# Moving ten of sixteen K transposes from TensorE to the DMA crossbar, and halving the chunk extremes in fp16

## The chip, the cores and the metric

The kernel runs on one core of one Trainium2 chip. Times are device microseconds (us) of one execution. The profile is taken on one of those executions; its span (first to last instruction) is some 2 us shorter than the device time. TensorE, VectorE, ScalarE, GpSimd and SyncE are the engines; in profile lines they are PE (PEld is its weight loads), DVE, ACT, POOL and SP. A letter q after an engine's name is its queue issuing something. "L170" is a source line. The changed kernel's line numbers are those of the kernel before plus 7, past the change.

## The reference, cut to what matters

```
q, k, v: (4, 8, 768, 64) float32     # batch, heads, rows, head size
k_min, k_max = min and max of k over chunks of 32 rows        # 24 chunks
ub  = sum_d max(q*k_min, q*k_max)        # bound per query row and chunk, causal chunks only
sel = the 6 chunks of largest bound
attn = softmax(q k^T / 8, masked to sel and to the causal triangle) ;  x = attn v
x -> (4, 768, 512)                       # heads side by side
h = relu(x @ w_in);  u, v = halves of h;  v_n = layer norm of v
out = (u * (w_spatial @ v_n + b_spatial)) @ w_out
```

## The kernel before

Sixteen pairs of heads pass through the attention part, and the second part ("MLP" below, one round per batch entry of four pairs) is woven between them. Each pair's K (768 rows x two heads of 64) lies in SBUF with rows on partitions and must be transposed: the chunk extremes are reductions along rows, and the scores need it as an operand.

```python
ps_ml = ctx.enter_context(tc.psum_pool(name="ps_ml", bufs=3))   # shared with the MLP

def k_transpose(self):
    if self.i < 16:                                   # all pairs
        self.kT = kT = ps_ml.tile([P, S], F16, tag="mlp", name="kTp")
        for t in range(NQT):                          # 6 blocks of 128 x 128
            nc.tensor.transpose(kT[:, t * P:(t + 1) * P], self.k[:, t], identity)
    else:
        self.kT = sb.tile([P, S], F16, tag="kT", name="kT", bufs=3)
        nc.sync.dma_start_transpose(out=..., in_=...)  # K rows x (6 blocks) -> kT

def k_max(self):                                      # k_min likewise, negated
    nc.vector.tensor_reduce(self.kmm[:, 0, :], self.kT.rearrange("d (c ch) -> d c ch", ch=CHUNK),
                            axis=AX.X, op=Alu.max)

def k_operand(self, hi):                              # two copies per pair: the scores' operand
    ...
    copy(self.kh[hi][d0:d1], self.kT[d0:d1])

# [...] already on the DMA crossbar, in SyncE's queue: a (selection and queries, pairs >= 8),
#       xT (attention result, pairs 4 to 14), gT (gated MLP values). The out stores stand there too.

def triangle(self, hi):                               # pairs >= 4: causal triangle on GpSimd
    if self.b == 0: return
    ...
    nc.gpsimd.affine_select(out=blk, in_=blk, compare_op=Alu.is_ge, fill=0.0, ...)

# [...] all loads are issued by GpSimd too: they cast float32 to fp16
tiles["k", g] = sb.tile([P, 2, NQT, 2, D], F16, tag="k", name="k", bufs=3)
nc.gpsimd.dma_start(out=t[...], in_=source(k, b, h, 2))               # pieces of 64 fp16 = 128 bytes
nc.gpsimd.dma_start(out=ws_raw[:, j], in_=moe_w_spatial[j*P:(j+1)*P]) # pieces of 768 fp16 = 1536 bytes
nc.gpsimd.dma_start(out=w_out_sb[:, j], in_=moe_w_out[j*P:(j+1)*P])   # pieces of 1024 bytes
```

In the traces below each engine's instructions run in the order of the program. And the profile counts all the transfers on the same 16 DMA engines of the core.

The softmax here doesn't subtract the row's maximum and nothing guards it: scores larger than these inputs give would overflow.

## Time and profile before

| | before |
|---|---|
| device time, median of 3 | 208.53 us (208.47 to 208.60) |
| profiled span, granted clock | 206.9 us, 1.0 in every slice of the page |

The page's first part gives busy time, share of the span and instructions of each engine.

```profile
PE 187.8 (91%) x1922; PEld 115.1 (56%) x1922; DVE 154.5 (75%) x454; ACT 158.1 (76%) x326; POOL 80.5 (39%) x100
```

The table by stretches gives for each stretch its length, the busy time of each engine with its instruction count, the granted TensorE clock, the time of the DMA packets as a share of 16 engines (over 1 where packets overlap), and last the GB/s that DMA moved.

```profile
core 0: us, PE busy (x) PEld busy (x) DVE busy (x) ACT busy (x) POOL busy (x), PEclk, DMA share, GB/s
57.00:77.00 20.00, 19.39 (x248) 13.47 (x247) 18.72 (x66) 17.68 (x38) 11.39 (x13) 1.00 1.84 134
77.00:97.00 20.00, 20.00 (x221) 12.39 (x220) 18.62 (x54) 15.52 (x33) 8.72 (x10) 1.00 1.84 135
97.00:122.00 25.00, 25.00 (x252) 14.89 (x251) 21.70 (x65) 23.44 (x53) 5.37 (x6) 1.00 1.40 176
122.00:152.00 30.00, 30.00 (x309) 17.82 (x308) 24.09 (x75) 23.82 (x51) 5.18 (x6) 1.00 0.64 122
```

From 77 us TensorE (first number after the length) is busy 75 of 75 us: here only less TensorE work would help. The same view for the time of the loads:

```profile
38.00:50.00 12.00, 10.72 (x171) 8.13 (x168) 10.99 (x39) 11.47 (x24) 9.15 (x12) 1.00 1.77 170
50.00:62.00 12.00, 11.06 (x145) 7.57 (x144) 10.60 (x33) 11.28 (x25) 11.28 (x14) 1.00 2.10 170
62.00:78.00 16.00, 15.45 (x191) 10.56 (x188) 15.02 (x52) 13.73 (x30) 7.39 (x8) 1.00 1.74 127
```

TensorE is not full from 38 to 50 us.

The groups by shape (busy us, mean ns of one, then idle time before and what ended it) show what the change touches: the transposes of K, the maximum, and the copies.

```profile
L170 PE MATMUL kTp<-identity,k 128*128 128x128 f16 x96 | 8.8, 230 | 5.9 <-DMA k<-in_k_dram 5.7
L178 DVE TENSOR_REDUCE kmm<-kTp 128x24 f16<-128x768 f16 x16 | 15.2, 948 | 3.7 <-PE kTp L170 2.7 <-ACT e L271 0.7
L194 DVE COPY kh<-kTp 64x768 f16<-64x768 f16 x30 | 16.5, 549 | 0.5
```

In the page's list of DMA issues the fourteen large K loads have a median of 8.1 us from issue to landing.

### The profile page before, as it was taken

How to read it: one execution, taken by the hardware profiler on the slowest of the kernel's cores; microseconds unless marked ns; L12 is line 12 of the kernel's file. 1: busy time of each engine (PE TensorE's matmuls, PEld its weight loads, DVE VectorE, ACT ScalarE, POOL GpSimd, SP SyncE). 2: the span in 40 equal slices, each digit the busy share in tenths (PEclk: the TensorE clock that was granted, in tenths of full speed). 3: DMA queues.
4: the chain of work that ended last, by engine and by line, in shares of the span. 5: the costliest groups of instructions: out<-in, count | busy, mean ns of one | idle time of the engine just before them, and what ended most of it. 6: DMA issues, size and time to landing. Idle time of an engine off the chain costs nothing.

```text
span 206.9 us, 5068 instructions
## 1 busy us (share of the span) xinstructions
PE 187.8 (91%) x1922; PEld 115.1 (56%) x1922; DVE 154.5 (75%) x454; ACT 158.1 (76%) x326; POOL 80.5 (39%) x100
## 2 busy tenths in 40 slices
PE   0368999898899999999999999999999999999992
PEld 0266776775666665656655656565555454444440
DVE  6467979989799989899797999887647456365520
ACT  4797989899998889785989996669999830666042
POOL 7997659596992463236114111111111110000000
PEclk9999999999999999999999999999999999999999
DMA  5999999999999999979998926648782124540356
GB/s 38 92 118 154 140 178 158 173 177 167 177 162 162 97 119 128 135 130 147 149 278 153 180 62 57 127 88 158 181 166 65 38 29 92 187 152 3 72 128 256
DMA packets 114424, 27.27 MB, mean 132 GB/s; under 512 B 109536, under 2 KB 110816, under 8 KB 114400
## 3 DMA queue, kind: packets, MB, share of 16 engines
q0 software_dynamic: 76544, 12.20, 89.8%
q1 hardware_dynamic: 37856, 14.75, 36.4%
q8 instruction: 15, 0.25, 0.5%
q14 instruction: 9, 0.07, 0.1%
HBM read 24.38 MB, written 6.29 MB: 148 GB/s over the span
## 4 chain that ended last, share of the span: by engine, by line
PE 69%; ACT 17%; DVE 8%; issue 2%; DMA 2%; POOL 0%; DVEq 0%; ACTq 0%; POOLq 0%
PE mlp L388 40%; PE sc L266 12%; ACT e L271 10%; PE acc L289 7%; PE kTp L170 2%; ACT a L257 2%; DVE kmm L178 2%; PE ub L222 2%; DMA k<-in_k_dram 2%; PE trm L251 2%; ACT vraw L398 1%; PE tr L205 1%; DVE vn L412 1%; DVE kmm L182 1%; ACT u L420 1%
## 5 line engine op out<-in xcount | busy, mean ns | idle before, releaser
L271 ACT ACTIVATE e<-sc 128x512 f16<-128x512 f32 x192 | 96.9, 553 | 14.8 <-PE sc L266 13.4
L266 PE MATMUL sc<-a,kh 128*128 128x512 f16 (+3 forms) x256 | 65.5, 308 | 2.1 <-ACT e L271 1.5
L388 PE MATMUL mlp<-w_in_sb,xT 128*128 128x512 f16 x192 | 53.0, 379 | 0.1
L278 POOL TENSOR_SCALAR_AFFINE_SELECT e<-e 128x768 f16<-128x768 f16 x24 | 20.9, 869 | 66.3 <-ACT e L271 66.3
L289 PEld LDWEIGHTS <-e 128*128 128x128 f16 x672 | 31.4, 97 | 17.0 <-DVE x L297 3.8
L388 PE MATMUL mlp<-vn,wsT 128*128 128x512 f16 x144 | 37.3, 379 | 0.0
L289 PE MATMUL acc<-vt,e 128*128 128x65 f16 x672 | 35.3, 193 | 0.7 <-DVE x L297 0.4
L266 PEld LDWEIGHTS <-kh 128*128 128x128 f16 x256 | 22.7, 98 | 13.3 <-issue 0.8
L437 ACT COPY o<-mlp 128x512 f32<-128x512 f32 x24 | 14.1, 586 | 19.5 <-PE mlp L388 19.1
L400 DVE BATCH_NORM_STATS2 stats<-vraw 128x6 f32<-128x512 f32 x24 | 16.6, 693 | 12.9 <-ACT vraw L398 12.5
L388 PE MATMUL mlp<-w_out_sb,gT 128*128 128x512 f16 x96 | 25.1, 379 | 0.0
L388 PEld LDWEIGHTS <-xT 128*128 128x128 f16 x192 | 17.2, 97 | 12.6 <-issue 0.4
L427 DVE SCALAR_TENSOR_TENSOR g<-mlp,b_col,u 128x512 f16<-128x512 f32 x24 | 17.9, 748 | 7.3 <-PE mlp L388 6.2
L232 DVE MAX8 max<-ub 128x8 f32<-128x8 f32 (+4 forms) x160 | 15.6, 165 | 5.1 <-PE ub L222 4.9
L388 PEld LDWEIGHTS <-wsT 128*128 128x128 f16 x144 | 12.9, 98 | 10.4
L178 DVE TENSOR_REDUCE kmm<-kTp 128x24 f16<-128x768 f16 x16 | 15.2, 948 | 3.7 <-PE kTp L170 2.7
L297 DVE TENSOR_TENSOR x<-acc,rec 128x384 f16<-128x384 f32 x32 | 17.6, 551 | 0.4
L336 POOL DMA_DIRECT2D qs<-in_q_dram x14 | 14.6, 1049 | 5.9 <-PE sc L266 5.9
L194 DVE COPY kh<-kTp 64x768 f16<-64x768 f16 x30 | 16.5, 549 | 0.5
L398 ACT ACTIVATE vraw<-mlp 128x512 f32<-128x512 f32 x24 | 14.4, 601 | 3.0 <-PE mlp L388 3.0
L420 ACT ACTIVATE u<-mlp 128x512 f16<-128x512 f32 x24 | 14.3, 598 | 1.7 <-PE mlp L388 1.5
L327 POOL DMA_DIRECT2D k<-in_k_dram x14 | 14.4, 1045 | 2.5 <-PE kTp L170 1.8
(67 smaller groups left out, 230.2 us busy)
## 6 DMA issues: line engine op xcount, KB each, us to landing
out_dram<-o SPq DMA_DIRECT2D x24, 256.0 KB, 2.3
vt<-in_v_dram POOLq DMA_DIRECT2D x8, 384.0 KB, 8.8
k<-in_k_dram POOLq DMA_DIRECT2D x14, 192.0 KB, 8.1
qs<-in_q_dram POOLq DMA_DIRECT2D x14, 192.0 KB, 7.5
ws_raw<-in_moe_w_spatial_dram POOLq DMA_DIRECT2D x6, 192.0 KB, 6.9
w_in_sb<-in_moe_w_in_dram POOLq DMA_DIRECT2D x8, 128.0 KB, 6.9
w_out_sb<-in_moe_w_out_dram POOLq DMA_DIRECT2D x4, 128.0 KB, 7.9
k<-in_k_dram POOLq DMA_DIRECT2D x4, 96.0 KB, 3.4
```

The costliest lines, as they stand in the source:

```text
L178: nc.vector.tensor_reduce(self.kmm[:, 0, :], self.kT.rearrange("d (c ch) -> d c ch", ch=CHUNK), axis=AX.X, op=Alu.max)
L194: copy(self.kh[hi][d0:d1], self.kT[d0:d1])
L266: mm(sc[:, col:col + n], lhsT=self.kh[hi][:, t * P:(t + 1) * P], rhs=self.a[:, q0 // P:(q0 + n) // P, hi, :], start=True, stop=not diag)
L271: nc.scalar.activation(out=self.e[hi][:, g * 512:g * 512 + width], in_=sc[:, 0:width], func=Act.Exp, scale=scale)
L278: nc.gpsimd.affine_select(out=blk, in_=blk, compare_op=Alu.is_ge, fill=0.0, base=0, channel_multiplier=-1, pattern=[[0, NQT], [1, P]])
L289: mm(self.av[:, qi, :], lhsT=self.e[hi][:, c:c + P], rhs=self.v[hi][:, t, 0:D + 1], start=first and n == 0, stop=last and n == len(blocks) ...
L297: nc.vector.tensor_tensor(self.x16[:, :, hi, :], in0=self.av[:, :, 0:D], in1=rec.to_broadcast([P, NQT, D]), op=Alu.mult)
L388: mm(st[group][:, 0:cols], lhsT=lhsT, rhs=rhs, start=(j == 0), stop=(j == n - 1))
L398: nc.scalar.activation(st["vraw"][:, ti, :], h, func=Act.Relu)
L400: nc.vector.bn_stats(stats, st["vraw"][:, ti, :])
L420: nc.scalar.activation(st["u"][:, ti, :], h, func=Act.Relu)
L427: nc.vector.scalar_tensor_tensor(g, in0=vs, scalar=b_col[:, ti:ti + 1], in1=st["u"][:, ti, :], op0=Alu.add, op1=Alu.mult)
```

## The change

The intent: K of pairs 6 to 15 is transposed by the DMA crossbar into SBUF, which frees TensorE of 60 transposes and a PSUM buffer of that use. From SBUF in fp16, the extremes of a chunk of 32 are taken by two elementwise halvings, 32 to 16 to 8, before a reduction over 8.

```diff
         def k_transpose(self):
-            if self.i < 16:
+            if self.i < 6:
                 self.kT = kT = ps_ml.tile([P, S], F16, tag="mlp", name="kTp")
 ...
         def k_max(self):
             self.kmm = sb.tile([P, 2, NCH], F16, tag="kmm", name="kmm")
-            nc.vector.tensor_reduce(self.kmm[:, 0, :], self.kT.rearrange("d (c ch) -> d c ch", ch=CHUNK),
-                                    axis=AX.X, op=Alu.max)
+            self.k_bound(0, Alu.max)
+
+        def k_bound(self, m, op):
+            src = self.kT.rearrange("d (c ch) -> d c ch", ch=CHUNK)
+            if self.i >= 6:
+                for n in (16, 8):
+                    half = sb.tile([P, NCH, n], F16, tag=f"half{n}", name=f"half{n}")
+                    nc.vector.tensor_tensor(half, in0=src[:, :, 0:n], in1=src[:, :, n:2 * n], op=op)
+                    src = half
+            nc.vector.tensor_reduce(self.kmm[:, m, :], src, axis=AX.X, op=op, negate=(m == 1))
 
         def k_min(self):
-            nc.vector.tensor_reduce(self.kmm[:, 1, :], ...same view..., op=Alu.min, negate=True)
+            self.k_bound(1, Alu.min)
```

## The prediction

> **What bounds the kernel now.** The time is 208.53 us, the profiled span 206.9 us, the granted clock 1.0 throughout. The table by stretches shows two regimes. Until about 55 us TensorE is not full (18.6 of 20 us busy from 20 to 40, 14.9 of 17 from 40 to 57), while VectorE (18.4 and 14.9) and ScalarE (17.9 and 16.2) are; the chain of waits alternates there between exponentials, reductions and transposes. From 57 us on TensorE is busy 19.4 of 20 us, then 20 of 20 in each stretch to 152, and the chain of waits is nearly all the MLP's and the scores' matmuls. Those run at pipeline pace: two 128x512 matmuls take 0.43 us in the chain. The matmuls of the stretch 77 to 152, added up at such paces (0.055 us for a transpose, 0.033 for a value matmul), give about 75 us of 75: TensorE throughput is the limit. The end (172 to 203 us) is MLP alone.
>
> **What the change does.**
> - It removes 60 of the 96 K transposes from TensorE. A record shows 219 ns, but six in a row take 0.33 us in the timeline, so 10 pairs x 0.33 = 3.3 us of TensorE time. Pairs 6 and 7 transposed at 45.8 and 53.7 us, in the regime where TensorE is not full; pairs 8 to 15 lie in the full one: 8 x 0.33 = 2.6 us, at par.
> - It frees a PSUM buffer that the MLP shares with the K transposes; TensorE shows no waits for these, so little.
> - VectorE: each 768-wide reduction from PSUM is 0.95 us, two per pair. They become 384- and 192-wide fp16 halvings and a 192-wide reduction. The Trainium skill (VectorE: DVE Perf Modes, "The perf-mode tier table") gives reduce 1x and a 16-bit SBUF tensor_tensor 2x. The trace's 948 ns fits 768 elements at 0.96 GHz (800) plus 148. My estimate on that base is 0.35 + 0.25 + 0.35 = 0.95 us per extreme at worst, 0.7 with a smaller SBUF overhead: a small gain. The two K copies (0.55 us from PSUM) should become about 0.35 us from SBUF. Together 0.4 to 0.9 us less VectorE per pair of about 3.0.
> - It adds ten 196 KB crossbar transposes to the SP queue. Those of x of the same size land in 4.2 us median, up to 8.8 beside the loads. The built order puts five ahead of the first x transpose; with three destination buffers they wait for the K copies three pairs earlier, which the order puts early enough. Slack is some 20 us against under 9: no stall. DMA load rises by about 2 MB of 27 in the crowded first 100 us; K loads arrive well ahead.
>
> **On the critical path.** Of 3.3 us removed, 2.6 lie in the full regime; the built order moves about 1 us of other TensorE work behind the first MLP matmul, but VectorE relief from 45 to 77 us may return it. Expected gain 2 to 3.5 us.
>
> **Prediction.** 205.7 us, 204.0 to 207.8 (8 in 10); faster by over 2%: 0.15, within 2%: 0.82, slower by over 2%: 0.03.
>
> **What would show it.** Right: TensorE still 20 of 20 from 77 us, its busy transposes of K gone, the MLP tail of about 31 us unchanged but starting 2 to 3 us earlier; K extremes' VectorE time equal or slightly less; K copies near 0.35 us; no matmul waiting on kT, a or xT. Wrong: a stall of ScalarE or TensorE on the a transposes (SP head-of-line), halvings slower than 0.35 us, new TensorE gaps from 57 to 100 us because loads or transposes land late, or a gain over 4 us from the freed PSUM buffer.

## The result, and the profile after

| | before, same chip | after |
|---|---|---|
| device time, median | 208.56 us (208.47 to 209.13, 4 runs) | 224.45 us (222.68 to 226.71, 4 runs) |
| profiled span, granted clock | 206.9 us, 1.0 | 222.4 us, 0.974 |

The ratio is 1.073, with a 95% interval of 1.069 to 1.077. Ratios here are the mean time of one kernel's fast runs over that of the other's of the same rounds, so not quite the ratio of the quoted medians. One run of the changed kernel, 226.71 us, counts as slow and is not in the ratio.

The page's first part, after:

```profile
PE 189.4 (85%) x1862; PEld 113.1 (51%) x1862; DVE 151.9 (68%) x494; ACT 158.4 (71%) x326; POOL 80.8 (36%) x100
```

There are 60 matmuls fewer, as intended, but PE busy has not fallen: part of the work ran at half clock (see below). The stretches, in the same columns as before:

```profile
57.00:77.00 20.00, 15.99 (x184) 10.71 (x185) 14.84 (x59) 13.88 (x28) 15.20 (x17) 0.91 2.02 167
77.00:97.00 20.00, 17.69 (x196) 10.70 (x195) 19.18 (x65) 15.46 (x38) 6.39 (x7) 1.00 1.90 147
97.00:122.00 25.00, 19.25 (x188) 10.75 (x186) 19.03 (x74) 17.25 (x39) 6.92 (x7) 1.00 1.39 161
```

TensorE, which should have stayed full, is idle for 4.0 us of 57 to 77, 2.3 of 77 to 97 and 5.75 of 97 to 122. The stretches of the loads:

```profile
38.00:50.00 12.00, 9.37 (x145) 6.72 (x142) 8.78 (x33) 10.21 (x21) 7.21 (x9) 1.00 1.46 128
50.00:62.00 12.00, 6.77 (x76) 4.62 (x73) 5.45 (x23) 5.64 (x13) 6.63 (x8) 0.80 2.42 158
62.00:78.00 16.00, 15.82 (x190) 10.61 (x189) 15.17 (x59) 14.65 (x30) 11.13 (x13) 0.94 2.04 162
```

DMA moves 128 GB/s from 38 to 50 us where the kernel before moved 170, although there is more to move. TensorE works 6.77 us of the next 12, and at a granted clock of 0.80.

VectorE's groups of the change, by shape:

```profile
L185 DVE TENSOR_TENSOR half<-kT 128x384 f16<-128x384 f16 x20 | 7.2, 367 | 6.6 <-DMA kT<-k 6.6
L185 DVE TENSOR_TENSOR half<-half 128x192 f16<-128x192 f16 x20 | 6.3, 324 | 0.0
L187 DVE TENSOR_REDUCE kmm<-half 128x24 f16<-128x192 f16 x20 | 6.7, 341 | 0.1
L201 DVE COPY kh<-kT 64x768 f16<-64x768 f16 x20 | 9.4, 471 | 0.3
```

The median landing time of the K loads has gone from 8.1 to 10.3 us, that of the w_spatial loads from 6.9 to 11.7.

Where does the time go? A good ruler is the start of each triangle selection in GpSimd's timeline, because the 24 of them come in the same order in both kernels.

| triangle selection | before | after | delay |
|---|---|---|---|
| first | 52.9 | 59.9 | 7.0 |
| fourth | 66.1 | 74.0 | 8.0 |
| eighth | 87.3 | 96.1 | 8.8 |
| twelfth | 107.3 | 117.9 | 10.7 |
| thirteenth | 112.2 | 128.6 | 16.5 |
| twenty-fourth | 167.5 | 183.1 | 15.6 |

The delay comes in two jumps, at the first selection and between the twelfth and thirteenth, with a little growth between. After the second jump it no longer grows. The MLP alone at the end lasts 31.53 us in the chain of waits of both kernels.

**First jump.** The chain of waits (start, length, what) runs through a K load and GpSimd's queue to the triangle selection, and only then to TensorE's value matmuls:

```profile
42.76 14.18 DMA k<-in_k_dram
...
57.23 0.37 POOL k L334
...
58.44 1.42 POOL vt L350
...
59.92 0.87 POOL e L285
...
60.83 0.51 PE acc L296 x6
```

The load of k issued at 42.8 us took 14.18 us. The kernel before issued the same load at the same time, and it landed after 7.5 us. The view of waits from 40 to 66 us says who waited (in total, times, longest):

```profile
PEld L296 <- POOL e L285: 5.6, 1, 5.6
PE acc L296 <- POOL e L285: 5.1, 1, 5.1
```

What was new in the machine then: the K transposes of pairs 6 and 7, issued at 38.0 and 39.4 us, which landed only at 48.8 and 52.3 us. The DMA packet records from 38 to 50 us show whom they met: a 1536-byte packet of a w_spatial load took 262 ns on average, against 142 ns before. The typical packet was no slower (median 134 ns, 135 before); 73 of the 362 took over 300 ns, up to 2.1 us, where the kernel before had 4 of 496. So a few packets were held for long. The 128-byte packets of the other loads took 34 and 32 ns on average.

**Second jump.** The chain of waits, later:

```profile
100.00 7.52 DMA gT<-g
...
115.02 0.23 SPq L445
...
115.35 2.86 DMA kT<-k
118.23 0.76 DVE half L185
...
122.13 0.47 DVE x L304
...
122.65 0.66 PE acc L296 x9
```

A gT transpose takes 7.52 us to land. Then pair 15's K transpose starts at 115.35, after an out store (SPq L445); VectorE waits for it; TensorE gets x at 122.6. SyncE's timeline (start, length, what) shows the queue, in which three gT transposes stood from 104.96 on:

```profile
110.23 4.38 SPq L253 DMA_TRANSPOSE a<-qs  x1
114.71 0.54 SPq L445 DMA_DIRECT2D out_dram<-o  x1
115.35 1.26 SPq L173 DMA_TRANSPOSE kT<-k  x1
```

Pair 15's K transpose was behind a selection transpose whose issue held the queue for 4.38 us, and behind the store.

**Half clock.** The records of the granted clock show three windows of 3.4 us at 0.5 in the changed kernel, from 50.3, 60.5 and 121.9 us, each after a gap in TensorE's work. The Trainium skill ("TensorE: Matmul & The Clock Gate", Part 1, the HAM clock gate) tells of windows of 3.4 us and a half clock after an idle one. This trace agrees for the second and third, before which TensorE did nothing for 3.4 us. Before the first it was busy for 1.5 of the 3.4 us, so here the clock fell without an idle window. TensorE was busy for 3.3, 3.1 and 2.7 us of the three, so half speed cost it at most about 9.0 x 0.5 = 4.5 us, by my estimate. So these gaps cost more than their own length.

### The profile page after: what moved, and what is told of

Its sections match the earlier page's. It is cut to its first block, busy times and chain, and to the rows that moved or that the text cites. A ratio compares the mean times of both kernels' runs of the same rounds, so it can differ in the third digit from the quotient of the medians.

```text
span 222.4 us, 5015 instructions
## 1 busy us (share of the span) xinstructions
PE 189.4 (85%) x1862; PEld 113.1 (51%) x1862; DVE 151.9 (68%) x494; ACT 158.4 (71%) x326; POOL 80.8 (36%) x100
## 4 chain that ended last, share of the span: by engine, by line
PE 50%; DVE 21%; DMA 12%; ACT 9%; issue 3%; POOL 2%; SPq 0%; DVEq 0%; POOLq 0%; ACTq 0%
PE mlp L395 31%; DMA k<-in_k_dram 8%; PE sc L273 7%; PE acc L296 6%; ACT e L278 5%; DVE kmm L187 5%; DMA gT<-g 3%; DVE vn L419 3%; DVE half L185 2%; DVE kh L201 2%; DVE x L304 2%; DVE max L239 2%; DMA kT<-k 1%; POOL vt L350 1%; PE ub L229 1%
## 5 line engine op out<-in xcount | busy, mean ns | idle before, releaser
L273 PE MATMUL sc<-a,kh 128*128 128x512 f16 (+3 forms) x256 | 68.0, 316 | 1.0 <-ACT e L278 0.6
L395 PE MATMUL mlp<-w_in_sb,xT 128*128 128x512 f16 x192 | 53.8, 380 | 0.0
L296 PE MATMUL acc<-vt,e 128*128 128x65 f16 x672 | 36.1, 196 | 15.2 <-DVE x L304 9.7
L273 PEld LDWEIGHTS <-kh 128*128 128x128 f16 x256 | 23.2, 100 | 13.2 <-issue 1.2
L395 PE MATMUL mlp<-w_out_sb,gT 128*128 128x512 f16 x96 | 25.9, 388 | 0.0
L239 DVE MAX8 max<-ub 128x8 f32<-128x8 f32 (+4 forms) x160 | 15.9, 162 | 5.7 <-PE ub L229 5.4
L395 PEld LDWEIGHTS <-wsT 128*128 128x128 f16 x144 | 12.9, 97 | 10.7
L350 POOL DMA_DIRECT2D vt<-in_v_dram x8 | 11.5, 1437 | 14.5 <-PE sc L273 12.8
L405 ACT ACTIVATE vraw<-mlp 128x512 f32<-128x512 f32 x24 | 14.3, 595 | 2.8 <-PE mlp L395 2.5
L427 ACT ACTIVATE u<-mlp 128x512 f16<-128x512 f32 x24 | 14.3, 598 | 1.4 <-PE mlp L395 1.3
L419 DVE TENSOR_SCALAR vn<-vraw,mv,rstd 128x512 f16<-128x512 f32 x24 | 12.4, 566 | 2.2 <-ACT rstd L417 2.2
## 6 DMA issues: line engine op xcount, KB each, us to landing
k<-in_k_dram POOLq DMA_DIRECT2D x14, 192.0 KB, 10.3
qs<-in_q_dram POOLq DMA_DIRECT2D x14, 192.0 KB, 10.3
ws_raw<-in_moe_w_spatial_dram POOLq DMA_DIRECT2D x6, 192.0 KB, 11.7
```

Of the source, the lines that this page charges most:

```text
L239: nc.vector.max(self.max8[:, qi - 1, hi, :], ub[:, c0:c0 + CPT * (qi + 1)])
L273: mm(sc[:, col:col + n], lhsT=self.kh[hi][:, t * P:(t + 1) * P], rhs=self.a[:, q0 // P:(q0 + n) // P, hi, :], start=True, stop=not diag)
L296: mm(self.av[:, qi, :], lhsT=self.e[hi][:, c:c + P], rhs=self.v[hi][:, t, 0:D + 1], start=first and n == 0, stop=last and n == len(blocks) ...
L395: mm(st[group][:, 0:cols], lhsT=lhsT, rhs=rhs, start=(j == 0), stop=(j == n - 1))
L419: nc.vector.tensor_scalar(st["vn"][:, ti, :], in0=st["vraw"][:, ti, :], scalar1=st["mv"][:, ti, 0:1], scalar2=st["rstd"][:, ti, :], op0=Al ...
```

## The experiments

Theory A says that the transposes do harm on the DMA side: by being in flight, they delay the loads. Rival B says that the consumers do it: they wait for kT, or the halvings are slow. A was later split: A1 is transposing beside wide load pieces, A2 the extra bytes and their place in the queues, A3 transposing beside loads of any width. D is the rival that transposes anywhere in the program cost time. Eighteen runs were made. All results were correct unless said otherwise. The kernel before, run beside them, took 208.62 to 209.03 us.

### The transposes without a reader, and the halvings alone

e1: the kernel before, plus the ten DMA transposes into tiles that nobody reads.

```diff
-            if self.i < 16:
+            if True:                      # TensorE path for all pairs
+            if self.i >= 6:
+                unread = sb.tile([P, S], F16, tag="kT", name="kT", bufs=3)
+                nc.sync.dma_start_transpose(out=unread..., in_=self.k...)
```

> The kernel before, with the ten DMA transposes of K added into a tile that nobody reads; TensorE still transposes all sixteen pairs, VectorE still reduces from PSUM. Theory A (the DMA side: transposes issued from 38 us on share the 16 DMA engines with the loads, loads land in 14 instead of 8 us, the GpSimd queue stands behind them and the triangle selection of pair 4 comes 7 us late): at least +5 us, 213 to 222, the first triangle selection at 58 to 60 us instead of 52.9. Theory B (the consumer side: VectorE's new order and the halvings cost the time): no change, 208 to 210.

Measured: 223.67 us (223.22 to 224.82), ratio 1.072 [1.069, 1.075]. The first triangle is at 59.5 us (+6.6). The whole loss of the change is there with nobody reading a transpose, so B falls as the main cause. The second half of it is spent differently: with no reader there is no step between the twelfth and thirteenth selections (+15.1 at both). The step is earlier instead, at the ninth (+14.3), where the selection transpose of pair 9 stood in SyncE's queue behind later K transposes and was issued at 100.5 us instead of 86.9.

e3: the changed kernel with the plain 768-wide reductions.

```diff
-            if self.i >= 6:
+            if False:                     # no halvings
```

> The changed kernel with the plain 768-wide reductions (from SBUF) in place of the halvings. Theory A: as slow as the changed kernel, 220 to 228. Theory B (halvings or their order cost the time): most of the 16 us come back, 208 to 214.

Measured: 221.42 us (220.61 to 222.20), ratio 1.061 [1.057, 1.064]. It is 3 us faster than the changed kernel, and 12.7 us of loss remain. The halvings are not the main cause, but they bring nothing. With them goes part of the second jump (more on this at the end of the experiments).

e4: DMA transposes from pair 10 on, where the first ones come after most loads.

```diff
-            if self.i < 6:
+            if self.i < 10:
 ...
-            if self.i >= 6:
+            if self.i >= 10:
```

> The changed kernel with DMA transposes and halvings only from pair 10 on, so that no K transpose can start before the loads of pairs 10 and 11 land (59 us before), after the w_spatial loads. Theory A: the 7 us lost before 61 us are gone; 206 to 212. Theory B: six tenths of the loss stays, about 218.

Measured: 218.96 us (218.58 to 219.98), ratio 1.050. The time is what B expected, but the loss does not lie where B has it. The first three selections are on time (53.2, 56.0, 61.9 us). The fourth is 8.3 us late. The view of waits from 56 to 80 us names the reason, a new kind of wait: a K load that needs a K buffer which a slow transpose still reads.

```profile
POOL k L334 <- DMA kT<-k: 9.5, 1, 9.5
```

e5: the changed kernel with the triangle of pairs 4 to 7 masked on TensorE, so that GpSimd's queue no longer gates the values there.

```diff
-                diag = self.b == 0 and si == 0
+                diag = self.i < 8 and si == 0
 ...
-            if self.b == 0:
+            if self.i < 8:
                 return
```

> The changed kernel, but the causal triangle of pairs 4 to 7 is added by TensorE in PSUM as for pairs 0 to 3, so that GpSimd's queue of loads holds nothing that TensorE waits for until pair 8. It costs TensorE 48 more 128-column matmuls, 48 x 0.055 = 2.6 us. If the 7 us before 61 us come through GpSimd's queue (theory A's last link): the gap of 5 us before the value matmuls at 60.8 us is gone and the time falls to 217 to 222. If TensorE really lacks the loaded data (rival C: the late loads themselves are missed), the gap stays in another place and the time is 224 to 229.

Measured: 228.78 us (227.85 to 229.42), ratio 1.096, as rival C expected. The stall moved to VectorE, as the view of waits from 56 to 80 us shows: a K load took 13.98 us to land, its transpose 7.79 us more, and VectorE waited for that. GpSimd's queue is one way in which late data hurts, not the source.

```profile
PE acc L296 <- DVE x L304: 6.2, 2, 5.9
DVE half L185 <- DMA kT<-k: 6.0, 1, 6.0
```

### What kind of traffic does the harm

e6: as e1, with plain copies of the same bytes in 256-byte pieces in place of the transposes.

```diff
-                nc.sync.dma_start_transpose(out=unread..., in_=self.k...)
+                nc.sync.dma_start(out=unread[:, :, 0:P], in_=self.k.rearrange("p t h d -> p t (h d)"))
```

> The kernel with ten unread K transposes, but each is a plain copy of the same 196 KB in pieces of 256 bytes (into a padded tile nobody reads), on the same queue and in the same order of instructions. Theory A1 (it is the transposing that slows the DMA engines beside the loads): the copies land in 2 to 5 us, the loads in at most 10 us, and the time is 208 to 213. Theory A2 (any 2 MB more in 256-byte packets in the crowded stretch does it): 218 to 225, as with the transposes.

Measured: 217.38 us (214.72 to 217.81), ratio 1.038 [1.031, 1.045], between the two expectations. The trace is of the fastest of the four runs. The first triangle is at 54.5 us (+1.6), and the loads from 38 to 50 us did well, as the stretch shows:

```profile
38.00:50.00 12.00, 10.72 (x170) 8.09 (x167) 10.99 (x39) 11.47 (x24) 8.79 (x11) 1.00 1.69 185
```

Plain copies do not make the first jump. But about half of the total loss remains, most of it in a step near 98 us: the extra transfers and their place in SyncE's queue are enough for that part.

e7: the unread transposes of pairs 6 and 7 only (`if self.i in (6, 7)`).

> The kernel before with the unread DMA transposes of pairs 6 and 7 alone, the two issued at 38 us beside the w_spatial loads. Theory A: the first triangle selection is 6 to 7 us late as with all ten, and with most of it kept to the end the time is 214 to 217. If the loss is spread over all ten evenly: 15 x 2/10 = 3 us, 211 to 212.

Measured: 216.71 us (215.33 to 217.60), ratio 1.037. The first triangle is at 58.4 us, and from the fourth on the delay is a constant 6.8 us. Two transposes among the loads make the first jump and nothing else. Their stretch:

```profile
38.00:50.00 12.00, 10.72 (x162) 7.96 (x159) 10.98 (x40) 11.46 (x25) 7.91 (x10) 1.00 1.47 136
```

e8: seven extra unread transposes of x between 104 and 163 us, away from the loads.

> The kernel before with seven more transposes of the same 196 KB that nobody reads, of the normalised output of pairs 8 to 14, issued right behind the ones that are there, from 104 to 163 us, where nearly all loads have landed. Theory A (a transpose hurts beside the loads): each lands in under 4 us and the time is 208 to 210. Rival D (a DMA transpose costs the same anywhere, through the SP queue or the SBUF): 7/10 of the loss, 215 to 220.

Measured: 208.71 us (208.63 to 208.74), ratio 0.999 [0.997, 1.001]. There these transposes are free, and D falls.

e9: e4 with four K buffers instead of three and six kT buffers instead of three.

> DMA transposes and halvings from pair 10 on as before in this study (218.96 us), with 4 instead of 3 K load buffers and 6 instead of 3 transposed-K buffers, so that no load in GpSimd's queue waits for a K transpose to land and no K transpose waits for a K copy. The 9.5 us wait of GpSimd's load for the K transpose at 62 to 72 us must vanish; if that wait carries the loss from there on, 207 to 212; if the slowed loads alone carry it, 215 to 219.

Measured: 213.89 us (213.63 to 214.80), ratio 1.025, between the two expected ranges. The 9.5 us wait of e4 is gone, and the first eight selections are on time. The ninth is 2.5 us late and the rest up to 5.3.

e10 and e11: the kernel before with the w_spatial loads replaced by loads of the same bytes from q, in 128-byte pieces (e10, a wrong result), and the same with the unread transposes of pairs 6 and 7 (e11, also wrong).

```diff
-        nc.gpsimd.dma_start(out=ws_raw[:, j], in_=moe_w_spatial[j * P:(j + 1) * P, :])
+        nc.gpsimd.dma_start(out=ws_raw[:, j].rearrange("p (x d) -> p x d", d=D), in_=source(q, 0, j, 2))
```

> Control for the next run, with a wrong result on purpose: the kernel before with the six w_spatial loads (768 values to a partition in one piece) replaced by loads of the same number of bytes from q, which land in pieces of 128 bytes. No theory expects more than a small change: 207 to 212, first triangle selection within 2 us of 52.9.

> The same narrow loads (wrong result on purpose) with the unread DMA transposes of pairs 6 and 7 beside them. Theory A1 (DMA transposes beside wide load pieces hold both up: beside the 1536-byte pieces a load packet took 262 instead of 142 ns on average): here no packet takes much longer, the transposes land in under 9 us, the first triangle selection is at most 3 us later than in the control, and the time is at most 4 us over it. Rival A3 (transposes beside any loads): 6 to 8 us over the control, as with the wide loads.

Measured: e10 208.63 us (208.26 to 208.70), e11 210.46 us (210.24 to 210.80). The two transposes cost 1.8 us here against 7.7 us in e7 (216.71 less 209.03 of its control): beside wide pieces they cost more. The stretch from 38 to 50 us, first e10, then e11:

```profile
38.00:50.00 12.00, 10.72 (x173) 8.17 (x170) 10.96 (x40) 11.47 (x24) 10.55 (x10) 1.00 2.21 159
```

```profile
38.00:50.00 12.00, 10.71 (x176) 8.27 (x174) 10.96 (x39) 11.40 (x23) 10.55 (x10) 1.00 1.92 154
```

### A version that wins?

e12: DMA transposes for pairs 12 to 15 only, with plain reductions. Each transpose is held back until pair i-5 has its result (a one-column copy into kT), and its readers until pair i-4 has.

> An attempt to beat both kernels: DMA transposes for pairs 12 to 15 alone, each held back until the normalisation of the pair five before it (from 92 us on, when most loads have landed), its readers on VectorE held back until the normalisation of the pair four before it, and plain reductions. TensorE saves 4 x 0.33 = 1.3 us. If theory A holds and nothing waits for these transposes: 206.8 to 208.3. If transposes still disturb what runs from 92 us on: 208.5 to 212.

Measured: 211.90 us (210.72 to 213.40, 6 runs), ratio 1.015 [1.012, 1.019]. It loses 3 us from 108 us on, where K's transpose and the gT and a transposes of the time land late together.

e13: the same from pair 13.

> The same from pair 13 on, so the first held-back transpose starts at about 101 us: TensorE saves 3 x 0.33 = 1.0 us. Theory A: 207.2 to 208.3; otherwise 208.5 or more.

Measured: 209.36 us (209.00 to 209.82, 6 runs), ratio 1.003 [1.002, 1.005]. Three pairs would give 3 x 0.33 = 1.0 us back to TensorE, and the kernel gains nothing.

### Narrow loads in the changed kernel: a theory falls

After e11 it looked as if the width of the load pieces were the cause. f1 puts that to the changed kernel, with a correct result: w_spatial is laid out so that it lands in 256-byte pieces. f3 is its control without the change, and f2 is f1 with more buffers.

```diff
-    ws_raw = cp.tile([P, NQT, S], F16)
+    ws_raw = cp.tile([P, NQT, NQT, P], F16)
 ...
-        nc.gpsimd.dma_start(out=ws_raw[:, j], in_=moe_w_spatial[j * P:(j + 1) * P, :])
+        nc.gpsimd.dma_start(out=ws_raw[:, :, j], in_=moe_w_spatial[...].rearrange("p (so s) -> p so s", s=P))
 ...
-            nc.tensor.transpose(tr[...], ws_raw[:, to, so * P:(so + 1) * P], identity)
+            nc.tensor.transpose(tr[...], ws_raw[:, so, to], identity)
 # f2 and f4 only:
-    ... tag="k", name="k", bufs=3        tag="kT", name="kT", bufs=3
+    ... tag="k", name="k", bufs=4        tag="kT", name="kT", bufs=6
```

> The changed kernel, but w_spatial is laid out in SBUF so that each load lands in 256-byte pieces instead of 1536-byte ones; same bytes, correct result, same order of instructions. If wide pieces beside the transposes of pairs 6 and 7 make the first loss (A1), the first triangle selection is at 53 to 55.5 us instead of 59.9, no load packet between 38 and 50 us averages over 100 ns, and the time is about 217 us (215 to 220). If the first loss comes from the transposes' own bytes or from the consumers, the first triangle stays at 59 to 60 us and the time within 1% of 224.5.

> The control: the kernel before with only the narrow w_spatial layout. 208 to 209.5 us under every theory; if it is under 207 or over 210, f1 and f2 are to be read against it and not against the kernel before.

Measured: f1 225.31 us (224.14 to 226.76), f3 208.87 us (208.47 to 209.33). The first selection came at 50.6 us, only 0.2 later than in f3, as A1 would have it. The time did not follow: the fourth selection is 8.4 us later than in the kernel before (8.2 later than in f3), with f1's chain of waits showing the same pattern one station further on.

```profile
56.10 15.74 DMA vt<-in_v_dram
...
74.45 0.89 POOL e L285
...
75.39 0.36 PE acc L296 x6
```

This load of v was issued at 56.1 us, when the transposes of pairs 8 and 9 (issued 57.5 and 58.8) and the w_out loads came. So the jump is not tied to one kind of load piece. The stretch from 38 to 50 us, first f3, then f1:

```profile
38.00:50.00 12.00, 10.72 (x176) 8.25 (x172) 10.96 (x40) 11.44 (x24) 9.40 (x10) 1.00 1.99 165
```

```profile
38.00:50.00 12.00, 10.79 (x165) 7.78 (x163) 10.70 (x44) 11.62 (x25) 9.03 (x10) 1.00 1.88 143
```

DMA still lost speed. By my reading the first selection was early only because that loss now fell on loads which it does not wait for.

> f1 with four K buffers instead of three and six buffers instead of three for the transposed K. If the later loss is K loads and K transposes that wait for buffers, the time falls to 209 to 213 us. If it is the bytes, or the order in SyncE's queue, the time stays within 2 us of f1.

Measured: f2 221.65 us (220.99 to 223.87), ratio 1.064. The fourth selection is again 8.5 us late, so buffers are not what that loss waits for. f2 does lack the second jump: pair 15's K transpose is issued at 96.4 us instead of 115.3, and the delay goes from 12.9 us at the twelfth selection to 14.2 at the thirteenth, where f1 goes from 11.1 to 16.5. In exchange K transposes now stand in front of the selection transposes. Pair 8's is issued at 93.2 us (84.6 in f1), and 5.3 us are lost between the eighth and ninth selections.

f4: f2 with the K transposes issued by ScalarE instead of SyncE.

> f2 with the K transposes issued by ScalarE instead of SyncE, so that nothing in SyncE's queue stands behind them. If that queue's order makes what f2 still loses, f4 is 2 to 5 us faster than f2, and the selection transposes of pairs 8 and on are issued as early as in the kernel before. If it is DMA traffic, f4 is within 1 us of f2; if ScalarE then waits itself for K loads ahead of its exponentials, f4 is slower than f2.

Measured: 232.26 us (231.61 to 234.34), ratio 1.115, the slowest of all. The first selection comes at 57.9 us, 7.3 later than in f1. ScalarE's timeline shows why: from 37.7 us on, the issues of two K transposes held its queue for 6.58 us.

In f4's trace no transpose of one engine starts before the other engine's has landed (K lands at 68.7 us and x starts at 68.8; K lands at 92.9 and x starts then). The Trainium skill ("DMA: Bandwidth & Descriptors", Rules for kernel authors) demands this order between transposes of different queues, and the built kernel keeps it. So f4 adds waits of its own and is no clean test of SyncE's order. What it shows beyond that: its delay stays at 23 to 24.5 us from the sixth selection to the end, without either late step.

### The crowd of loads taken away

Theory C, formed after f1: until about 62 us the loads of the kernel before have no time to spare, and each transpose among them sets the whole train back. g1 is the changed kernel without the loads of w_spatial and w_out, both tiles filled with a constant by VectorE at the start (wrong result). g2 is the kernel before with the same edit.

```diff
-        nc.gpsimd.dma_start(out=ws_raw[:, j], in_=moe_w_spatial[...])     # and the same for w_out
+        pass
 ...
+        nc.vector.memset(ws_raw, 0.01); nc.vector.memset(w_out_sb, 0.01)  # in the setup
```

> The changed kernel without the loads of w_spatial and w_out (1.7 MB in fp16, landed between 38 and 70 us); both tiles are filled with a constant by VectorE at the start, so the result is wrong on purpose and the start shifts by a few us, as in the control. Theory C (the crowd of loads is the cause up to some 90 us): the triangles are within 1.5 us of the control's up to 87 us, and the time is within 2% of g2, 0 to 4 us above it, what is left coming from after 90 us. If queue orders (SyncE, GpSimd, VectorE) make the loss without a crowd, g1 stays 12 to 16 us above g2.

> The control: the kernel before without those loads, wrong on purpose in the same way. Every theory: 206 to 212 us, since its loads were in time already and the two fills cost the start some us.

Measured: g1 225.19 us (223.86 to 226.05), g2 216.41 us (216.30 to 216.53). The fills cost the start more than I had reckoned: the first attention result comes at 31.8 us instead of 24.1 in both, so the two are compared with one another alone. Their selections:

| triangle selection | g2 | g1 | delay |
|---|---|---|---|
| first | 58.0 | 58.4 | 0.4 |
| third | 67.5 | 70.2 | 2.7 |
| fourth | 73.8 | 72.7 | -1.1 |
| eighth | 95.0 | 96.4 | 1.4 |
| twelfth | 115.0 | 116.6 | 1.6 |
| thirteenth | 119.9 | 129.1 | 9.2 |
| twenty-fourth | 175.2 | 183.6 | 8.4 |

The first jump is gone (only the third selection is outside the 1.5 us expected), and with it the growth up to the twelfth. The second jump is there whole, so my expectation of 0 to 4 us in total was wrong: 8.8 us remain, nearly all from one place. The stretches show why the first part is free here, first g2, then g1:

```profile
38.00:50.00 12.00, 10.91 (x167) 8.03 (x165) 11.89 (x42) 11.09 (x24) 9.89 (x12) 1.00 2.04 156
50.00:62.00 12.00, 10.06 (x157) 7.62 (x154) 9.90 (x30) 11.64 (x27) 3.27 (x3) 1.00 1.47 78
```

```profile
38.00:50.00 12.00, 10.92 (x167) 8.13 (x166) 11.89 (x42) 11.09 (x25) 6.56 (x9) 1.00 1.88 155
50.00:62.00 12.00, 10.88 (x153) 7.74 (x151) 10.76 (x40) 11.86 (x29) 9.11 (x10) 1.00 2.80 138
```

The transposes slow g1's loads too, but its control has a stretch at 78 GB/s, in which g1 moves 138 and catches up. In the real kernel that stretch runs at 170 GB/s and leaves less room. (170 is no ceiling of DMA: e6 moved 185 from 38 to 50 us.) The waits of g1 from 112 to 124 us, at the second jump:

```profile
DVE half L185 <- DMA kT<-k: 5.8, 1, 5.8
PE acc L296 <- DVE x L304: 4.3, 1, 4.3
```

It is the same picture as in the changed kernel: pair 15's K transpose was issued at 115.1 us after an out store. This part needs no crowd of loads. It goes with a K transpose late in SyncE's queue and a reader: g1, f1 and the changed kernel have both and show the jump; f2 issues it early and e1 has no reader, and neither shows it. But e3 has both too (pair 15's transpose issued at 117.8 us) and loses less by it: VectorE waits for it 2.0 us, TensorE for x 2.1, and the delay grows by 2.1 us between the thirteenth and fourteenth selections. Another 3.2 us are lost just before, at the twelfth, where the chain holds an xT transpose that took 10.02 us to land. So the size of the jump depends on more than these two conditions, and no run takes it apart.

## Why the prediction was wrong, point by point

The prediction was 205.7 us (204.0 to 207.8), with 3% for slower by over 2%. The kernel took 224.45 us.

- *TensorE is the limit from 57 us on*: right for the kernel before. The lesson is that a full engine only stays full while its data is in time.
- *60 transposes, 3.3 us of TensorE, 2.6 at par*: the count is right (1922 to 1862 matmuls). After the second jump the delay shrinks from 16.5 to 15.6 us over the last pairs; that may be a little of this gain, but no run isolates it. e13 shows nothing of the 1.0 us it should have brought.
- *Extremes 0.95 us at worst, K copies near 0.35*: right for the undisturbed instruction, too low for the mean. The means of the three records add to 0.367 + 0.324 + 0.341 = 1.03 us against 0.948 before, and they partly overlap. The copies take 0.471 us on average, not 0.35, against 0.549. VectorE's busy time fell from 154.5 to 151.9 us. The Trainium skill ("VectorE: DVE Perf Modes", The perf-mode tier table) has the reduction at 1x and the 16-bit elementwise operation at 2x. The medians of the records agree with what I worked out from that: 344 ns for the 384-wide halving (my 0.35), 248 for the 192-wide one (0.25), 340 for the reduction (0.35), and 357 for a copy (0.35). So even undisturbed, three short instructions cost as much as the one they replace. What raises the means is a minority of slow records, which the trace finds beside GpSimd's work. The five 192-wide halvings that overlap a triangle selection took 442 to 645 ns, the other fifteen 236 to 293; copies that overlap nothing on GpSimd took 317 to 358 ns, while six of the eight that overlap a selection or a load's issue took 441 to 1005. In the kernel before, VectorE read K from PSUM, and its reductions (919 to 958 ns) and copies (508 to 562) were no slower beside GpSimd. I had not reckoned with that; no run isolates it.
- *"Slack is some 20 us against under 9: no stall"* and *"K loads arrive well ahead"*: **this is the step that failed.** I compared one transpose's landing time with its own reader's slack, and even there both figures failed. The transposes of pairs 6 and 7 took 10.8 and 12.9 us instead of under 9, and VectorE was ready for the first 8.2 us after its issue, not 20: it waited 2.7 us for it, and TensorE 1.75 us for x behind it. But that is not what set the delay, since with no reader at all (e1) the first selection is still 6.6 us late, against 7.0. The harm was to the loads around the transposes, whose slack I never asked for: a K load that had landed after 7.5 us now took 14.2. DMA ran at a steady 170 GB/s from 38 to 62 us, and I read it as "crowded" and counted bytes: 2 MB more of 27.
- *What would show it wrong*: the note named "new TensorE gaps from 57 to 100 us because loads or transposes land late" and the head of SyncE's queue. The gaps came. SyncE's queue did harm too, but not as I had named it: neither TensorE nor ScalarE has a wait for a selection transpose in the changed kernel's view of waits; VectorE waits 3.9 us for pair 15's K transpose. "Slower by over 2%" had been given a chance of 3%.

How much do two transposes take from the loads? They write 2 x 196,608 bytes, which is 33 GB/s over the 12 us from 38 to 50. That share, taken from the GB/s of the stretch, leaves the loads' rate (for the changed kernel slightly too low, since pair 7's transpose landed at 52.3 us):

| load pieces of w_spatial | GB/s without | GB/s with two transfers | of it loads | lost by the loads | lost per added byte |
|---|---|---|---|---|---|
| 1536 bytes (before, changed kernel) | 170 | 128 | 95 | 75 | 2.3 |
| 1536 bytes (before, e7) | 170 | 136 | 103 | 67 | 2.0 |
| 256 bytes (f3, f1) | 165 | 143 | 110 | 55 | 1.7 |
| 128 bytes (e10, e11) | 159 | 154 | 121 | 38 | 1.2 |
| 1536 bytes, plain copies (before, e6) | 170 | 185 | 152 | 18 | 0.5 |

So in these stretches a transposed byte took the room of 1.2 to 2.3 load bytes, more the wider the loads' pieces, and a copied byte half of one. Part of the 1536-byte figures may be loads that GpSimd issued later because it was itself waiting.

The sum of the 15.9 us, as far as it is shown: about 7 us are the train of loads set back by the transposes among them (e7 has it alone, g1 lacks it). About 6 to 8 us are the second jump (5.8 us in the changed kernel, 7.6 in g1), where the chain of waits shows pair 15's K transpose late in SyncE's queue with VectorE and TensorE behind it; this cause is read from the traces and not isolated by a run. The rest, some 2 us up to the eighth selection and 2 us from there to the twelfth, less 0.9 us regained at the end, is not taken apart; the second of these comes where gT, a, xT and K transposes land together. The half-clock windows are inside these numbers, not on top. The Trainium skill says that DMAs of different issuers end on the same 16 DMA engines ("DMA: Bandwidth & Descriptors", Issuing engines are not separate DMA queues). This agrees: SyncE's transposes doubled the landing time of GpSimd's k load from 7.5 to 14.2 us.

Open: why the crossbar transposes and wide load pieces hold one another up was not shown, only that they do. Open too is why the issue of one selection transpose holds SyncE's queue for 4.38 us. Whether another order of SyncE's queue alone would bring the second part back was not cleanly tested, since f2 moved the loss and f4 added waits. No version beat the kernel before.

## What to carry to other kernels

Before you move work to DMA, ask of the stretch where it will land whether the present transfers have room. Here a stretch with the same GB/s as its neighbour, followed by one with less, was a train with little slack, and transposes inserted there delayed what stood behind them; one kernel is no rule, but it is a sign to look for. Ask for the slack of what is already there, not only of the new transfer's reader. And look at what stands in front of and behind the new instruction in its in-order queue: more buffers moved the late transpose forward and delayed others.

## What the Trainium skill lacked or had wrong

- "Advanced Engine Details and Errata", X-Bar Transpose (TRN2), says "TRN2 transpose DMAs are as fast as regular DMAs". Here that did not hold beside loads: with two transposes the stretch from 38 to 50 us moved 136 GB/s in all (e7), with plain copies of the same source bytes 185 (e6). Away from loads the transposes cost no time (e8, 208.71 us).
- "DMA: Bandwidth & Descriptors", Rules for kernel authors, says that a transpose next to ordinary DMAs needs nothing. All results with such neighbours were correct, save those made wrong, so this agrees for correctness. For speed it lacks a warning: the loads lost 1.2 to 2.3 bytes for each byte transposed beside them, and a 1536-byte load packet took 262 ns instead of 142 on average (the median stayed at 134, so a few were held for long).
- No page that I read says that the cost depends on the width of the neighbouring loads' pieces (two transposes cost 1.8 us beside 128-byte pieces in e11, 7.7 us beside 1536-byte ones in e7). In the changed kernel narrower pieces did not save time (f1, 225.31 us).
- No page that I read gives a trn2 figure for how long issuing a transpose can hold the issuer's queue: 4.38 us for one on SyncE in the changed kernel, 6.58 us for two on ScalarE in f4.
